# A retention layer feeding a gated two-layer block on one core: early loads of q, k, v put on another queue, and the first pairs' work reordered

## The chip, the cores and the metric

The kernel runs on one core of a Trainium2 chip. The core has five engines, each with its own queue that it works off in order: TensorE (PE, matrix products; its weight loads are shown apart as PEld), VectorE (DVE), ScalarE (ACT), GpSimd (POOL) and SyncE (SP, which only issues transfers here). Engines wait for each other through semaphores. Sixteen DMA engines carry the transfers of all queues. [...] The metric is the device time of one execution in microseconds, lower is better.

## What is computed

The inputs are q, k, v of shape (4, 8, 768, 64) and two weight matrices, all in float32. For each batch and head, a state is decayed and updated over 768 steps, and read with q. The result, 3072 tokens of 512 values, goes through two matrix products with an activation between them.

```python
gamma = 1.0 - 2.0 ** (-5.0 - np.arange(H))
for t in range(S):
    state = gamma * state + outer(k[:, :, t], v[:, :, t])
    y[:, :, t] = scale * (q[:, :, t] @ state)
x = y.transpose(0, 2, 1, 3).reshape(3072, 512)
h = x @ w_in            # 512 x 2048
g = h * np.cos(h)
out = g @ w_out         # 2048 x 512
```

## The kernel before, in words

The recurrence is done in chunks of 128 steps: six chunks for each batch entry. Two batch entries are worked side by side, which makes 12 **pairs** p = 0 to 11: pair p is chunk p mod 6 of batch entries b = 0 and 1 (p below 6) or 2 and 3. Two successive pairs give the 512 tokens of one **group** g of the block behind (six groups). "The second to fourth pairs" are p = 1, 2, 3.

A pair takes six loads of 256 KB: q0, q1, k0, k1, v0, v1 (the digit is b). `load` (L105) issues them on the queue that it is given, into five buffers for each (p mod 5). Then:

- `conv_q` (L150) and `conv_v` (L155) scale q and v with per-step factors and turn them to bfloat16, on the engine that they are given, two products a pair; `conv_k` (L160) copies k to bfloat16 on ACT, two copies a pair. There are three sets of buffers for these (p mod 3).
- `stage_t` (L167): PE transposes q and k (L176) into a PSUM bank for each b, and DVE or ACT copies the bank to `qkt` (L178, L180). From p = 5 on, transfers on SP do this instead (L186).
- `stage_a` (L196): PE makes the scores inside a chunk (L205). `stage_m` (L211, called by `masks`): DVE masks them into `am` (L214), four operations a pair.
- `stage_y` (L219): PE adds what the state gives (L228) and what the scores give (L233); ACT copies the result to `xt` (L237). Then PE updates the state (L245), and ACT or DVE copies it to `stb` (L250).

The block behind has `pair_f(p, r, parts)` (L272): for the 256 tokens of pair p and slice r of four, PE makes the first product in two halves of eight matmuls (L279); for each half, ACT takes the cosine into one of three buffers `cosb` (L258), and DVE multiplies into `gt` (L262). `parts` picks one half. Slice r needs slice r of w_in. From the third group on `unit_f` (L264) does the same for 512 tokens. `unit_o` (L288) is the second product, from `gt` and `w_out_sb`.

`load_w_in` (L114) and `load_w_out` (L119) load slices of the weights on POOL's queue, cast to bfloat16 on the way. Slice 0 of w_in is loaded in two parts of 256 columns, slices 1 to 3 as 512 columns each; w_out has four slices, which are all needed when `unit_o` begins.

Seven PSUM banks are taken and given back in rotation, one more is kept as `spare` for `warm(n)` (L313), which issues n matmuls that nobody reads, until `spare` is given to the rotation as well.

The schedule is manual: each engine works off its instructions in the order in which the program names them. Names follow the order of the code: L125 to L143 (first loads and constants), then L322 to L389 (the pairs 0 to 3 with all `pair_f`, written out by hand), then the loop at L393, in which `unit_f`, `unit_o` and the stages of pairs 4 to 11 alternate. A transfer reuses a semaphore that an earlier transfer of its queue had, and waits until that one has landed; there are eight for POOL's queue and eight for SP's.

Of the kernel before, what the change touches and what calls it, by code (L numbers as in the profile page):

```python
# [30 lines left out]
def kernel(  # L31
# [9 lines left out]
    nc = tc.nc  # L41
# [63 lines left out]
    def load(eng, p, names):  # L105
        bp, c = divmod(p, NC)
        for n in names:
            t, src = SRC[n[0]]
            b = int(n[1])
            eng.dma_start(  # L110
                out=t[p % PRE][b],
                in_=src[2 * bp + b, :, ds(c * C, C)].rearrange("h t d -> t h d"))

    def load_w_in(r, n=512):  # L114
        nc.gpsimd.dma_start(
            out=w_in_sb[:, :, ts(r, n)],
            in_=moe_w_in[:, ts(r, n)].rearrange("(i p) f -> p i f", p=128))

    def load_w_out(r):  # L119
        nc.gpsimd.dma_start(  # L120
            out=w_out_sb[:, ts(r, 4), :],
            in_=moe_w_out[ts(r, 512), :].rearrange("(f p) m -> p f m", p=128))
# [2 lines left out]
    nc.gpsimd.iota(pos, pattern=[[C, NC]], base=1, channel_multiplier=1,  # L125
                   allow_small_or_imprecise_dtypes=True)
    load(nc.sync, 0, ("q0", "k0", "q1"))
    load(nc.sync, 1, ("q0", "q1"))
    load(nc.gpsimd, 0, ("k1", "v0", "v1"))
    make_identity(nc, ident)  # L130
    nc.vector.memset(zero, 0.0)
# [15 lines left out]
    def bc(g, c):  # L147
        return g[:, c, :].unsqueeze(2).to_broadcast([128, H, D])

    def conv_q(p, eng):  # L150
        for b in range(2):
            eng.tensor_tensor(out=qs[p % NB][:, b], in0=qf[p % PRE][b],  # L152
                              in1=bc(gq, p % NC), op=ALU.mult)

    def conv_v(p, eng):  # L155
        for b in range(2):
            eng.tensor_tensor(out=vs[p % NB][:, b], in0=vf[p % PRE][b],  # L157
                              in1=bc(gk, p % NC), op=ALU.mult)

    def conv_k(p, on_act):  # L160
        for b in range(2):
            if on_act:
                nc.scalar.copy(out=ks[p % NB][:, b], in_=kf[p % PRE][b])  # L163
            else:
                nc.vector.tensor_copy(out=ks[p % NB][:, b], in_=kf[p % PRE][b])

    def stage_t(p, split, fill=0):  # L167
        n = p % NB
        for b in range(2):
            if fill:  # L170
                warm(fill * b)
            bank = banks.take()
            tr = bank.bitcast(BF16).rearrange("p (w a t) -> p w a t", w=2, a=HP)
            for w, src in enumerate((qs[n], ks[n])):
                for a in range(HP):
                    nc.tensor.transpose(tr[:, w, a, :], src[:, b, 2 * a : 2 * a + 2, :], ident)  # L176
            if split is None or split and b == 1:
                nc.vector.tensor_copy(out=qkt[n][:, :, b], in_=tr)  # L178
            else:
                nc.scalar.copy(out=qkt[n][:, :, b], in_=tr)  # L180
            banks.give(bank)
# [8 lines left out]
    def qt(n, b, a):  # L190
        return qkt[n][:, 0, b, a, :]

    def kt(n, b, a):
        return qkt[n][:, 1, b, a, :]

    def stage_a(p):  # L196
        n = p % NB
        todo = []
        for b in range(2):
            bk = [banks.take(), banks.take()]  # L200
            ap = [t.rearrange("p (a t) -> p a t", a=HP) for t in bk]
            for a in range(HP):
                for j in range(2):
                    po = 64 * j
                    nc.tensor.matmul(ap[j][:, a, :], lhsT=kt(n, b, a)[po : po + 64, :],  # L205
                                     rhs=qt(n, b, a)[po : po + 64, :],
                                     tile_position=(po, 0))
            todo.append((b, bk, ap))
        return todo

    def stage_m(p, item):  # L211
        b, bk, ap = item
        for j in range(2):
            nc.vector.tensor_tensor(  # L214
                out=am[p % 2][b][j], in0=ap[j],
                in1=mask.unsqueeze(1).to_broadcast([128, HP, 128]), op=ALU.mult)
            banks.give(bk[j])

    def stage_y(p, copy_st=nc.vector.tensor_copy):  # L219
        c = p % NC  # L220
        n = p % NB
        for b in range(2):
            bank = banks.take()
            yp = bank.rearrange("p (a t) -> p a t", a=HP)
            for a in range(HP):
                if c > 0:
                    for j in range(2):
                        nc.tensor.matmul(  # L228
                            yp[ts(j, 64), a, :], lhsT=stb[p % 2][:, b, a, ts(j, 64)],
                            rhs=qt(n, b, a), start=True, stop=False,  # L230
                            skip_group_check=True)
                for j in range(2):
                    nc.tensor.matmul(  # L233
                        yp[ts(j, 64), a, :], lhsT=vs[n][:, b, 2 * a + j, :],
                        rhs=am[p % 2][b][j][:, a, :], start=(c == 0), stop=True,
                        skip_group_check=True)
            nc.scalar.copy(out=xt[(p // 2) % 2][:, :, ts(2 * (p % 2) + b, C)], in_=yp)  # L237
            banks.give(bank)
        if c == NC - 1:
            return  # L240
        for b in range(2):
            for a in range(HP):
                for j in range(2):
                    h = 2 * a + j
                    nc.tensor.matmul(  # L245
                        st_ps[ts(j, 64), b, a, :], lhsT=ks[n][:, b, h, :],
                        rhs=vs[n][:, b, h, :], start=(c == 0 and b == 0 and a == 0),
                        stop=True, skip_group_check=True)
        for j in range(2):
            copy_st(out=stb[(p + 1) % 2][ts(j, 64), :, :, ts(j, 64)], in_=st_ps[ts(j, 64)])  # L250
# [4 lines left out]
    def act(bank, out):  # L255
        cb = cosb[f_no[0] % 3]
        f_no[0] += 1
        nc.scalar.activation(out=cb, in_=bank, func=AF.Sin, bias=halfpi)  # L258
        if len(out.shape) == 3:
            cb = cb.rearrange("p (f t) -> p f t", f=2)  # L260
            bank = bank.rearrange("p (f t) -> p f t", f=2)
        nc.vector.tensor_tensor(out=out, in0=bank, in1=cb, op=ALU.mult)  # L262
# [9 lines left out]
    def pair_f(p, r, parts=(0, 1)):  # L272

        g, hf = divmod(p, 2)
        for f in [4 * r + 2 * i for i in parts]:
            bank = banks.take()
            for e in range(2):
                for i in range(KIN):
                    nc.tensor.matmul(bank[:, ts(e, 256)], lhsT=w_in_sb[:, i, ts(f + e, 128)],  # L279
                                     rhs=xt[g % 2][:, i, ts(hf, 256)],  # L280
                                     start=(i == 0 and e == 0), stop=(i == KIN - 1),
                                     skip_group_check=True)
            act(bank, gt[g % 2][:, f : f + 2, ts(hf, 256)])
            banks.give(bank)
# [28 lines left out]
    def warm(n):  # L313
        for _ in range(n):
            nc.tensor.matmul(spare, lhsT=zero[:, :128], rhs=zero, start=True, stop=True,
                             skip_group_check=True)

    def masks(p, items):
        for it in items:
            stage_m(p, it)  # L320

    load(nc.gpsimd, 1, ("k0", "k1", "v0", "v1"))  # L322
    load_w_in(0, 256)
    load_w_in(1, 256)
    for r in (1, 2, 3):
        load_w_in(r)
    for p in (2, 3, 4):
        load(nc.sync, p, ("q0", "q1", "v0"))
    conv_v(1, nc.gpsimd)
    load(nc.gpsimd, 2, ("k0", "k1", "v1"))  # L330
    load(nc.gpsimd, 3, ("k0", "k1"))
    conv_q(2, nc.gpsimd)
    load(nc.gpsimd, 3, ("v1",))
    load_w_out(0)
    conv_v(2, nc.gpsimd)
    load_w_out(1)

    warm(10)
    conv_q(0, nc.vector)
# [7 lines left out]
    conv_q(1, nc.vector)  # L347
    warm(6)
    stage_y(0, nc.scalar.copy)
    conv_q(3, nc.gpsimd)  # L350
    load_w_out(2)
    load_w_out(3)
    conv_v(3, nc.gpsimd)
    load(nc.gpsimd, 4, ("k0", "k1", "v1"))
    stage_t(1, None)
    m1 = stage_a(1)
    masks(1, m1)
# [1 line left out]
    banks.give(spare)  # L359
    stage_y(1, nc.scalar.copy)  # L360
    pair_f(1, 0)
    for r in (1, 2, 3):
        pair_f(0, r)
        pair_f(1, r)
    conv_k(2, True)
    stage_t(2, None)
    m2 = stage_a(2)
    masks(2, m2)
    stage_y(2, nc.scalar.copy)
    load(nc.sync, 5, ("q0", "q1", "v0"))  # L370
    conv_q(4, nc.gpsimd)
    load(nc.gpsimd, 5, ("k0", "k1", "v1"))
    pair_f(2, 0)
    conv_k(3, True)
    pair_f(2, 1)
    stage_t(3, None)
    pair_f(2, 2, (0,))
# [15 lines left out]
    for g in range(1, NG + 1):  # L393
        for s in range(16):
            hf, r = divmod(s, 8)
            p = 2 * (g + 1) + hf
# [52 lines left out]
```

## Time and profile before

| what | value |
|---|---|
| runs | 219.2 to 222.09 us, median 219.92 (6 runs) |
| profiled execution | 220.12 us, its span 218.4 us |
| PE busy | 203.6 us (93%), 1699 matmuls |
| DVE / ACT / POOL busy | 113.4 / 116.2 / 83.8 us |
| DMA, hardware queue of SP and ACT | 54640 packets, 19.01 MB |
| DMA, software queue of POOL | 7712 packets, 13.90 MB |
| HBM read / written | 27.26 / 6.29 MB |
| PE busy in 34 to 41 us | 4.26 of 7.00 us |
| PE busy in 41 to 53 us | 10.47 of 12.00 us |
| PE busy in 65 to 218 us | 149.43 of 153.00 us |

The span runs from the first to the last instruction; times inside it are counted from its start. The landing of a transfer is the time at which its semaphore tells that all of it has arrived. Where each early transfer landed, in us (p and name; the queue is SP's where marked, else POOL's):

| transfer | landed |
|---|---|
| p=1: q0 (SP), q1 (SP), k0, k1, v0, v1 | 8.7, 10.9, 10.1, 11.7, 13.0, 13.9 |
| w_in, 256 columns, twice; slices 1, 2, 3 | 15.9, 18.1; 21.7, 25.1, 28.4 |
| p=2: q0, q1, v0 (all SP); k0, k1, v1 | 16.4, 22.4, 29.9; 30.1, 30.9, 31.7 |
| p=3: q0, q1, v0 (all SP); k0, k1, v1 | 37.5, 41.6, 42.3; 32.6, 33.4, 34.2 |
| w_out, slices 0 to 3 | 37.7, 41.3, 51.3, 54.7 |
| p=4: q0, q1, v0 (all SP); k0, k1, v1 | 43.2, 44.1, 45.4; 55.5, 56.3, 57.1 |

PE's own milestones: `pair_f(0, 0)` starts at 17.95, `pair_f(1, 0)` at 21.61, `pair_f(2, 0)` at 40.67, `pair_f(3, 0)` at 52.41 and the first `unit_o` at 59.39.

### The profile page before, as it was taken

What the parts mean: (1) busy time and instruction counts of PE and PEld (TensorE: products, weight loads), DVE (VectorE), ACT (ScalarE), POOL (GpSimd) and SP (SyncE); (2) the same over time, 40 slices, a digit from 0 to 9 for tenths busy, and PEclk for the clock granted to TensorE, in tenths of its full rate; (3) what the DMA queues carried; (4) which work ended last, traced back from release to release, by engine and by line L of the source; (5) the groups of instructions that cost most, each with busy time, mean ns of one, the idle gap of its engine ahead of it and who ended that gap; (6) DMA issues with size and microseconds to landing.
All of it is one profiled execution on the core that took longest, in us unless ns stands there. A gap on an engine that the chain in (4) does not pass through costs nothing.

```text
span 218.4 us, 4269 instructions
## 1 busy us (share of the span) xinstructions
PE 203.6 (93%) x1699; PEld 112.6 (52%) x1699; DVE 113.4 (52%) x183; ACT 116.2 (53%) x185; POOL 83.8 (38%) x96
## 2 busy tenths in 40 slices
PE   7578996889999999999999999999999999999992
PEld 2246884768855454544544544544544544444440
DVE  4398588386663417557448547647546244333000
ACT  5654874748874274564474564564534644454120
POOL 7988432499599953958070600000000000000000
PEclk9799999999999999999999999999999999999999
DMA  6999999899999999997972651051011001110221
GB/s 155 332 245 195 204 321 212 178 177 239 300 269 236 269 188 283 283 299 125 271 194 59 140 144 48 3 144 50 3 48 48 22 29 48 48 50 3 96 84 60
DMA packets 62516, 33.31 MB, mean 153 GB/s; under 512 B 52320, under 2 KB 57184, under 8 KB 62496
## 3 DMA queue, kind: packets, MB, share of 16 engines
q1 hardware_dynamic: 54640, 19.01, 37.8%
q0 software_dynamic: 7712, 13.90, 26.3%
q8 instruction: 13, 0.21, 0.4%
q10 hardware_dynamic: 144, 0.13, 0.2%
q14 instruction: 7, 0.06, 0.1%
HBM read 27.26 MB, written 6.29 MB: 154 GB/s over the span
## 4 chain that ended last, share of the span: by engine, by line
PE 83%; DVE 6%; ACT 5%; DMA 3%; issue 1%; SPq 0%; DVEq 0%; ACTq 0%
PE bank L293 37%; PE bank L267 26%; PE bank L279 11%; DMA qf<-in_q_dram 3%; PE bank L205 3%; DVE am L214 2%; PE bank L228 2%; PE bank L233 2%; ACT cosb L258 1%; ACT ks L163 1%; DVE qkt L178 1%; DVE qs L152 1%; ACT xt L237 1%; PE bank L176 1%; DVE gt L262 1%
## 5 line engine op out<-in xcount | busy, mean ns | idle before, releaser
L262 DVE TENSOR_TENSOR gt<-bank,cosb 128x512 bf16<-128x512 f32 x96 | 65.9, 690 | 70.0 <-ACT cosb L258 69.9
L258 ACT ACTIVATE cosb<-bank,halfpi 128x512 bf16<-128x512 f32 x96 | 65.8, 687 | 60.0 <-PE bank L267 49.9
L293 PE MATMUL bank<-w_out_sb,gt 128*128 128x512 bf16 x384 | 94.3, 379 | 0.0
L267 PE MATMUL bank<-xt,w_in_sb 128*128 128x512 bf16 x256 | 65.8, 379 | 0.0
L293 PEld LDWEIGHTS <-gt 128*128 128x128 bf16 x384 | 37.2, 98 | 44.3
L267 PEld LDWEIGHTS <-w_in_sb 128*128 128x128 bf16 x256 | 24.1, 98 | 28.3
L214 DVE TENSOR_TENSOR am<-bank,mask 128x512 bf16<-128x512 f32 x48 | 30.2, 682 | 5.9 <-PE bank L205 3.4
L152 POOL TENSOR_TENSOR qs<-qf,gq 128x512 bf16<-128x512 f32 x20 | 20.6, 1047 | 27.5 <-DMA qf<-in_q_dram 20.3
L279 PE MATMUL bank<-xt,w_in_sb 128*128 128x256 bf16 x256 | 28.9, 273 | 1.4 <-ACT xt L237 1.4
L157 POOL TENSOR_TENSOR vs<-vf,gk 128x512 bf16<-128x512 f32 x22 | 23.0, 1064 | 12.3 <-DMA vf<-in_v_dram 10.0
L279 PEld LDWEIGHTS <-w_in_sb 128*128 128x128 bf16 x256 | 24.8, 98 | 4.4 <-issue 1.3
L305 ACT COPY ob<-bank 128x512 f32<-128x512 f32 x23 | 13.5, 586 | 16.3 <-PE bank L293 16.1
L110 POOL DMA_DIRECT2D kf<-in_k_dram x23 | 20.9, 911 | 0.4 <-issue 0.4
L237 ACT CAST xt<-bank 128x512 bf16<-128x512 f32 x24 | 13.1, 588 | 14.7 <-PE bank L233 14.7
L163 ACT CAST ks<-kf 128x512 bf16<-128x512 f32 x24 | 13.7, 616 | 2.5 <-DMA kf<-in_k_dram 2.5
L233 PE MATMUL bank<-am,vs 128*64 128x128 bf16 x192 | 12.2, 219 | 1.2 <-DVE am L214 1.1
L110 POOL DMA_DIRECT2D vf<-in_v_dram x14 | 12.4, 888 | 0.0
L250 DVE CAST stb<-st_ps 64x512 bf16<-64x512 f32 x12 | 8.3, 689 | 6.5 <-PE st_ps L245 6.3
L233 PEld LDWEIGHTS <-vs 128*64 128x64 bf16 x192 | 10.3, 110 | 1.7 <-issue 0.9
L228 PEld LDWEIGHTS <-stb 128*64 128x64 bf16 x160 | 8.7, 109 | 4.5 <-issue 4.2
L228 PE MATMUL bank<-qkt,stb 128*64 128x128 bf16 x160 | 10.6, 222 | 0.0
L205 PE MATMUL bank<-qkt 64*128 64x128 bf16 x192 | 8.4, 223 | 2.3 <-DVE qkt L178 1.9
(37 smaller groups left out, 68.5 us busy)
## 6 DMA issues: line engine op xcount, KB each, us to landing
qf<-in_q_dram SPq DMA_DIRECT2D x24, 256.0 KB, 6.7
kf<-in_k_dram POOLq DMA_DIRECT2D x23, 256.0 KB, 5.7
out_dram<-ob SPq DMA_DIRECT2D x23, 256.0 KB, 2.2
vf<-in_v_dram POOLq DMA_DIRECT2D x14, 256.0 KB, 6.4
vf<-in_v_dram SPq DMA_DIRECT2D x10, 256.0 KB, 7.2
w_out_sb<-in_moe_w_out_dram POOLq DMA_DIRECT2D x4, 512.0 KB, 9.9
w_in_sb<-in_moe_w_in_dram POOLq DMA_DIRECT2D x3, 512.0 KB, 14.3
w_in_sb<-in_moe_w_in_dram POOLq DMA_DIRECT2D x2, 256.0 KB, 8.0
```

What stands on the lines that cost most here:

```text
L110: eng.dma_start(out=t[p % PRE][b], in_=src[2 * bp + b, :, ds(c * C, C)].rearrange("h t d -> t h d"))
L152: eng.tensor_tensor(out=qs[p % NB][:, b], in0=qf[p % PRE][b], in1=bc(gq, p % NC), op=ALU.mult)
L157: eng.tensor_tensor(out=vs[p % NB][:, b], in0=vf[p % PRE][b], in1=bc(gk, p % NC), op=ALU.mult)
L163: nc.scalar.copy(out=ks[p % NB][:, b], in_=kf[p % PRE][b])
L214: nc.vector.tensor_tensor(out=am[p % 2][b][j], in0=ap[j], in1=mask.unsqueeze(1).to_broadcast([128, HP, 128]), op=ALU.mult)
L228: nc.tensor.matmul(yp[ts(j, 64), a, :], lhsT=stb[p % 2][:, b, a, ts(j, 64)], rhs=qt(n, b, a), start=True, stop=False, skip_group_check=True)
L233: nc.tensor.matmul(yp[ts(j, 64), a, :], lhsT=vs[n][:, b, 2 * a + j, :], rhs=am[p % 2][b][j][:, a, :], start=(c == 0), stop=True, skip_grou ...
L258: nc.scalar.activation(out=cb, in_=bank, func=AF.Sin, bias=halfpi)
L262: nc.vector.tensor_tensor(out=out, in0=bank, in1=cb, op=ALU.mult)
L267: nc.tensor.matmul(bank, lhsT=w_in_sb[:, i, ts(f, 128)], rhs=xt[g % 2][:, i, :], start=(i == 0), stop=(i == KIN - 1))
L279: nc.tensor.matmul(bank[:, ts(e, 256)], lhsT=w_in_sb[:, i, ts(f + e, 128)], rhs=xt[g % 2][:, i, ts(hf, 256)], start=(i == 0 and e == 0), s ...
L293: nc.tensor.matmul(bank, lhsT=gt[g % 2][:, f, ts(j, 128)], rhs=w_out_sb[:, f, :], start=(f == 0), stop=(f == KOUT - 1))
```

## The change

```diff
     load(nc.sync, 0, ("q0", "k0", "q1"))
-    load(nc.sync, 1, ("q0", "q1"))
+    load(nc.sync, 1, ("q0", "v0"))
     load(nc.gpsimd, 0, ("k1", "v0", "v1"))
...
-    load(nc.gpsimd, 1, ("k0", "k1", "v0", "v1"))
+    load(nc.gpsimd, 1, ("k0", "q1", "k1", "v1"))
     load_w_in(0, 256)
     load_w_in(1, 256)
-    for r in (1, 2, 3):
-        load_w_in(r)
-    for p in (2, 3, 4):
-        load(nc.sync, p, ("q0", "q1", "v0"))
+    load_w_in(1)
+    load(nc.sync, 2, ("q0", "q1"))
+    load(nc.sync, 4, ("q0", "q1", "v0"))
     conv_v(1, nc.gpsimd)
-    load(nc.gpsimd, 2, ("k0", "k1", "v1"))
-    load(nc.gpsimd, 3, ("k0", "k1"))
+    load_w_in(2)
+    load(nc.gpsimd, 2, ("k0", "k1"))
+    load_w_in(3)
+    load(nc.gpsimd, 2, ("v0", "v1"))
+    load(nc.gpsimd, 3, ("k0", "q0", "k1", "q1"))
     conv_q(2, nc.gpsimd)
-    load(nc.gpsimd, 3, ("v1",))
-    load_w_out(0)
     conv_v(2, nc.gpsimd)
-    load_w_out(1)
+    load(nc.gpsimd, 3, ("v0", "v1"))
+    for r in range(4):
+        load_w_out(r)
...
     stage_y(0, nc.scalar.copy)
-    conv_q(3, nc.gpsimd)
-    load_w_out(2)
-    load_w_out(3)
     conv_v(3, nc.gpsimd)
     load(nc.gpsimd, 4, ("k0", "k1", "v1"))
+    warm(2)
     stage_t(1, None)
...
     pair_f(1, 0)
-    for r in (1, 2, 3):
+    for r in (1, 2):
         pair_f(0, r)
         pair_f(1, r)
     conv_k(2, True)
+    pair_f(0, 3)
     stage_t(2, None)
+    pair_f(1, 3, (0,))
     m2 = stage_a(2)
     masks(2, m2)
+    pair_f(1, 3, (1,))
     stage_y(2, nc.scalar.copy)
...
     pair_f(2, 0)
     conv_k(3, True)
+    conv_q(3, nc.vector)
     pair_f(2, 1)
     stage_t(3, None)
```

On SP's queue, v0 of p = 1 takes the place of q1, and behind q0, q1 of p = 2 stand those of p = 4 at once; v0 of p = 2 and q0, q1, v0 of p = 3 have left it. On POOL's queue, q1 of p = 1 and six loads of p = 2 and 3 are new or moved: k of p = 2 stands between slices 2 and 3 of w_in, `conv_v(1)` before slice 2, and the four slices of w_out stand behind all loads of p = 3. `conv_q(3)` goes from POOL to DVE, behind the products of `pair_f(2, 0)`. On PE, the last slice of `pair_f` for p = 0 and 1 is spread over the stages of p = 2: `pair_f(0, 3)` before the transposes, one half of `pair_f(1, 3)` before the scores and one before `stage_y(2)`. ACT's `conv_k(2)` and DVE's `gt` products move with them. Two `warm` matmuls are added ahead of the transposes of p = 1. What is computed is the same.

## The prediction

> **What bounds the kernel now.** I read the page's busy shares first: PE is busy for 203.6 of the 218.4 us span. So I asked for PE's waits by stage, then the chain of waits through the stage where they lie, then the timelines of DVE and POOL for prices. The profiled execution took 220.12 us, 1.72 around its span, and 0.20 above the median of 219.92. The waits of PE between 21.7 and 53 us (total, times, longest):
>
> ```profile
> PE bank L205 <- DVE qkt L178: 1.5, 4, 0.9
> PE bank L279 <- ACT xt L237: 1.4, 3, 0.5
> PE bank L176 <- ACT ks L163: 1.1, 1, 1.1
> PE bank L233 <- DVE am L214: 0.8, 2, 0.4
> ```
>
> And from 53 us to the end:
>
> ```profile
> PE bank L205 <- ACT qkt L180: 0.4, 1, 0.4
> ```
>
> No row names a DMA. After 21.7 us PE never waits for a transfer directly, and after 53 us it hardly waits at all, so whatever shift of PE the change makes by 53 us reaches the end whole. What can be won there is 4.8 us. The chain of waits (start, length, what) for pair p=2 shows where most of it sits:
>
> ```profile
> 34.03 0.69 ACT cosb L258
> 34.72 0.51 ACT ks L163
> ...
> 35.28 0.41 PE bank L176 x4
> ...
> 35.72 0.55 DVE qkt L178
> ...
> 36.32 0.61 DVE qkt L178
> ...
> 37.53 1.88 DVE am L214 x3
> ...
> 40.04 0.59 ACT xt L237
> ...
> 40.67 2.79 PE bank L279 x24
> ```
>
> PE has finished every pair_f of p=0 and 1 at 33.83, and then ACT, PE and DVE hand the work of p=2 to each other until pair_f(2, 0) starts at 40.67. Prices come from these rows of the timelines (start, length):
>
> ```profile
> 13.86 2.29 DVE L152 TENSOR_TENSOR qs<-qf,gq 128x512 bf16<-128x512 f32 x2
> ...
> 45.00 1.29 DVE L262 TENSOR_TENSOR gt<-bank,cosb 128x512 bf16<-128x512 f32 x2 [0.92 <-ACT cosb L258]
> 46.21 1.28 DVE L178 COPY qkt<-bank 128x1024 bf16<-128x1024 bf16 x2
> ```
>
> ```profile
> 13.12 2.49 POOL L157 TENSOR_TENSOR vs<-vf,gk 128x512 bf16<-128x512 f32 x2 [0.82 <-DMA vf<-in_v_dram]
> ```
>
> A pair of DVE operations takes 1.29, but conv_q(1) took 2.29 while POOL ran conv_v(1), which itself took 2.49 where two lone ones take 2.05.
>
> **The loads that move.** On the software queue a load lands every 0.8 us when queued (p=2 and 3, from 30.1 to 34.2 us). On SP the loads issued at 12.1 and 16.4 us needed 25.4 and 25.1, those issued by POOL in the same stretch 14.3 to 14.6: between 20 and 28 us the two queues moved nearly equal packet counts (1222 and 1218), but 1.41 MB against 0.31. So q of p=3, at 37.5 and 41.6 before, lands by about 35. [...] What must hold is that no load becomes late.
>
> q, v of p=1 swap queues: v0 takes q1's SP place (landed 10.9, on POOL before 13.0), q1 lands in k1's POOL place (11.7; needed by DVE at 13.9), k1 in v0's (13.0, before 11.7; conv_k(1) then ends at 13.6, its transposes are at 16.2). conv_v(1) starts 2 us earlier for b=0, but b=1 still waits for v1 at 13.9 and then meets conv_q(1) on DVE as before. I take 0, with −0.9 (no meeting) to +0.2 as ends. warm(2) adds two matmuls (six took 1.47 with their latency, so some 0.5) where PE now waits 0.83 for conv_q(1): free, or +0.2 if conv_q(1) gets quicker; inside the same ends.
>
> w_in(2) is issued after conv_v(1), at about 15 to 16 instead of 10.8 us; the queue is occupied until w_in(1) lands at 21.7, so it still lands at 25.1 (needed 26.9). w_in(3) now stands behind two loads of k. Rows: 3.3 to 3.6 per w_in slice, 0.8 per queued load, but 1.7 for the first load after a slice. So 25.1 + 1.6 + 3.3 = 30.0 at best, and 25.1 + 1.7 + 0.8 + 4.2 = 31.8 if the slice pays that 0.9 too. pair_f(0, 3) needs it at 30.34. The cover is conv_k(2), which now holds ACT just then: up to 30.8 nothing is lost, beyond it each us is one. So 0 to +1.0; I take 0, nearer to the other row of this kind (behind the last slice of w_out, landed at 54.66, the next k landed 0.86 later).
>
> POOL holds at most eight transfers in flight: w_out(0) waited 1.4 until w_in(2), issued eight places earlier, had landed (25.09), and went at 25.75. By that rule q1 of p=3 leaves after k0 of p=2 lands (about 26), so conv_q(2) runs at 27.5 to 29.6, needed at 32.1; conv_v(2) waits for v (31 to 33.6) and ends by 34.7, needed at 36.5; v of p=3 and the four w_out follow (4.9 us of issue), w_out lands by about 54 (needed 59.4); conv_v(3) ends between 39.6 and 41.4, needed at 49; loads of p=4 take 2.7 more, so conv_q(4) starts between 42.3 and 44.1.
>
> **Pair 2 on PE.** conv_k(2) moves ahead of the last four half-units' cosines. Half-units follow each other every 0.87 on PE; the cosine of the tenth after 21.6 us ends at 31.23, where in the old order the fourteenth's ended at 34.72: 3.49 earlier. conv_k(2) ends at 32.25 instead of 35.74. PE runs pair_f(0, 3) to 32.1 and the transposes to 33.0, without waiting. The cosines of pair_f(0, 3) follow conv_k on ACT at 32.15, so its first gt starts at 32.87. From there DVE has gt, gt, qkt, qkt, gt, am: exactly the series of p=3 before, where am began 3.00 after the first gt (45.00 to 48.00). So am starts at 35.87, and pair_f(2, 0) follows am by 3.75 as before (36.92 to 40.67): 39.62, that is **−1.05**. The two halves of pair_f(1, 3) lie in waits that stay.
>
> **Pair 3 on DVE.** conv_q(3) leaves POOL for DVE, between the gts of pair_f(2, 0) and of pair_f(2, 1). Counted from pair_f(2, 0): before, the second gt ended at 3.41 and the next began at 4.33, after conv_k(3) and a cosine. Alone, the two products take 1.29 and end at 4.62; with spacing 0.6 the next gt begins at 4.53, and qkt, A, am follow **+0.2** later. But they start at 39.62 + 3.33 = 42.95, and POOL's conv_q(4) lies between 42.3 and 46.2. If they meet as conv_q(1) and conv_v(1) did, DVE needs 2.29: **+1.0** more (0 if POOL starts after 44; 1.4 if it starts just before DVE, 0.65 of waiting and then another 1.04 between the two products, less what was idle). I take the meeting, since most of POOL's interval gives it. [...] Behind conv_q(3) on DVE wait gt of pair_f(2, 1), qkt and am of p=3, and PE waits at L205 for them; pair_f(2, 2) and (2, 3) keep their length. The old conv_q(3) on POOL (37.70 and 41.71) ended before PE needed it, so its removal gives PE nothing.
>
> Sum: 0 − 1.05 + 0 + 0.2 + 1.0 = +0.15, on the span 218.55, on the median 220.1.
>
> **Rivals.**
> No meeting: POOL's conv_q(4) is over or begins late; −0.85 gives 219.1, with pair 1's −0.9 also 218.2. For it: POOL's interval is guessed within 2 us. Against: DVE's 1.3 us lie well inside it.
> w_in(3) late, the slower side: it decides from 30.8 us on. At 31.8 it costs 1.0: 221.1; with the meeting's upper end 221.5; over 222.1 it needs a landing at 32.8. For it: the 1.7 row. Against: the 0.86 row.
> The clock: PE was busy for 1.26 us in the stretch 4.57 to 7.99, and the granted clock was 0.50 in the next 3.41. If p=3's longer wait does that, half of 3.41 is lost: 221.8. Against: 34.0 to 37.4 had 1.87 busy and kept 1.00.
> Pair 2's waits vanish: all 2.7 us of waits between 34 and 40.7 go and only the 0.2 remains: 217.4. Against: gt and qkt still queue on DVE behind conv_k.
> The loads do nothing for PE: contained in all of these, at 0.
>
> **How the numbers follow.** Within 1% (217.7 to 222.1) is about what counts as no change here. Chances: forecast 0.38 (own range 219.5 to 220.7), no meeting 0.25, w_in late 0.18 (0.07 of it beyond 222.1), clock 0.09 (0.05 beyond), waits vanish 0.10 (0.07 below 217.7). Faster 0.07, same 0.81, slower 0.12. The range 218.3 to 221.9 leaves out the vanishing waits (0.10) and the upper parts of w_in and clock (0.10).
>
> **What would show it.** pair_f(2, 0) at about 39.6 us; DVE's two L152 products at about 43 with 2.2 to 2.7 us for both, beside POOL's L152; no PE wait at pair_f(0, 3) for w_in; the interval from pair_f(2, 0) to pair_f(3, 0), 11.74 before, at 12.9. I am wrong if PE waits for a DMA after 21.7 us, if the clock drops again, or if PE's waits after 53 us grow.

## The result, and the profile after

The changed kernel takes 220.0 us (median of 35 runs, 219.18 to 225.56), the kernel before 220.11 in the runs taken beside it (72 runs). The ratio is 0.9995, with a 95% interval from 0.9978 to 1.0013: no change that can be measured, at 220.0 where 220.1 was forecast. The profiled execution has a span of 218.6 us. The ratios leave out executions more than 1.5% above the fastest of their kernel (4 of 12 of e4, 7 of 12 of e5), and since the profiled execution of e5 and of e6 is such a one, only its rows ahead of 53 us are read.

PE's waits between 21.7 and 53 us in the changed kernel (total, times, longest):

```profile
PE bank L176 <- DVE qs L152: 1.2, 2, 0.8
PE bank L205 <- DVE qkt L178: 1.0, 4, 0.3
PE bank L279 <- ACT xt L237: 0.9, 2, 0.5
PE bank L279 <- DMA w_in_sb<-in_moe_w_in_dram: 0.7, 1, 0.7
PE bank L233 <- DVE am L214: 0.6, 2, 0.4
```

And from 53 us on:

```profile
PE bank L205 <- DMA qkt<-ks: 0.7, 1, 0.7
PE bank L205 <- ACT qkt L180: 0.4, 1, 0.4
```

Before, the four rows of the first stretch came to 4.8 us. They count a wait of 0.5 for xt that ends at 21.61, just ahead of `pair_f(1, 0)`; the changed kernel's rows leave the same wait out, since it ends at 20.84 there. So 4.3 us stand against the 4.4 of the five rows now. The wait for ks of p=2 (1.1) and a third of those for qkt (1.5, now 1.0) are gone; a wait for DVE's products qs (1.2) and one for w_in (0.7) stand in their place. In the second stretch a wait for a transposing transfer has come that was not there.

The chain of waits (start, length, what) shows both sides of the trade, p=2 first and p=3 below it:

```profile
30.43 1.94 PE bank L279 x16
...
32.38 0.70 ACT cosb L258
...
33.10 0.69 DVE gt L262
33.80 1.11 DVE qkt L178 x2
...
35.51 2.48 DVE am L214 x4
...
39.26 1.92 PE bank L279 x16
...
42.66 2.04 DVE qs L152 x2
44.70 1.20 DVE gt L262 x2
45.90 1.21 DVE qkt L178 x2
...
52.02 1.03 PE bank L279 x8
```

`pair_f(2, 0)` starts at 39.26 where it started at 40.67, and the two products qs stand in the chain of p=3 with 2.04 us. The same in intervals, read from the starts of the L279 matmuls:

| stretch | before | after | difference |
|---|---|---|---|
| start of `pair_f(1, 0)` | 21.61 | 20.84 | −0.77 |
| to `pair_f(2, 0)` | 19.06 | 18.42 | −0.64 |
| to `pair_f(3, 0)` | 11.74 | 12.76 | +1.02 |
| to the first `unit_o` | 6.98 | 6.98 | 0 |
| to the end of the span | 159.02 | 159.57 | +0.55 |

The last row holds the wait of 0.72 at 84.14 us. The first row turns out below not to come from the change.

### The profile page after: what moved, and what is told of

It reads as the page before. It is cut to its first block, busy times and chain, and to the rows that moved or that the text cites. A ratio compares the mean times of both kernels' runs of the same rounds, so it can differ in the third digit from the quotient of the medians.

```text
span 218.6 us, 4276 instructions
## 1 busy us (share of the span) xinstructions
PE 204.8 (94%) x1701; PEld 112.2 (51%) x1701; DVE 115.0 (53%) x185; ACT 116.2 (53%) x185; POOL 86.4 (40%) x98
## 4 chain that ended last, share of the span: by engine, by line
PE 70%; DMA 15%; DVE 5%; ACT 4%; POOL 3%; SPq 1%; issue 1%; DVEq 0%; ACTq 0%; POOLq 0%
PE bank L293 34%; PE bank L267 25%; DMA w_in_sb<-in_moe_w_in_dram 5%; DMA qkt<-ks 5%; PE bank L279 5%; DMA vf<-in_v_dram 4%; PE bank L205 2%; PE bank L233 2%; PE bank L228 2%; DVE gt L262 2%; ACT cosb L258 2%; POOL vs L157 1%; SPq L110 1%; DVE am L214 1%; DVE qkt L178 1%
## 5 line engine op out<-in xcount | busy, mean ns | idle before, releaser
L279 PE MATMUL bank<-xt,w_in_sb 128*128 128x256 bf16 x256 | 29.5, 273 | 2.1 <-ACT xt L237 1.4
L152 POOL TENSOR_TENSOR qs<-qf,gq 128x512 bf16<-128x512 f32 x18 | 19.1, 1079 | 23.8 <-DMA qf<-in_q_dram 18.4
L279 PEld LDWEIGHTS <-w_in_sb 128*128 128x128 bf16 x256 | 24.6, 98 | 5.4 <-issue 1.3
L237 ACT CAST xt<-bank 128x512 bf16<-128x512 f32 x24 | 13.0, 588 | 10.9 <-PE bank L233 10.9
L110 POOL DMA_DIRECT2D vf<-in_v_dram x15 | 13.4, 893 | 0.0
```

The lines of the kernel that those rows point to most:

```text
L110: eng.dma_start(out=t[p % PRE][b], in_=src[2 * bp + b, :, ds(c * C, C)].rearrange("h t d -> t h d"))
```

## The experiments

All ratios are to the kernel before, in runs on the same chip. "Interval 2" is from `pair_f(1, 0)` to `pair_f(2, 0)`, "interval 3" from there to `pair_f(3, 0)`.

**e1: conv_q(3) back on POOL.**

```diff
     stage_y(0, nc.scalar.copy)
+    conv_q(3, nc.gpsimd)
     conv_v(3, nc.gpsimd)
...
     conv_k(3, True)
-    conv_q(3, nc.vector)
     pair_f(2, 1)
```

> The changed kernel with conv_q(3) put back on POOL, ahead of conv_v(3). Theory (the two products on DVE meet POOL's conv_q(4) and cost about 1.0, the longer series on DVE 0.2): the interval from pair_f(2, 0) to pair_f(3, 0) falls from 12.76 to about 11.74, and the time by about 1.0 us (ratio to before about 0.995). Rival A (POOL is the scarce engine, DVE has room): the interval stays at 12.5 or more, because transposes of p=3 now wait for POOL. Rival B (what costs is the wait of 0.72 us for a transposing transfer at 84 us, made by the new order of the queues): that wait is here too and the total does not fall.

The starts of `pair_f(2, 0)` and `pair_f(3, 0)` in its PE timeline (start, length, what):

```profile
39.37 3.65 PE L279 MATMUL bank<-xt,w_in_sb 128*128 128x256 bf16 x32 [0.42 <-ACT xt L237]
...
51.10 3.11 PE L279 MATMUL bank<-xt,w_in_sb 128*128 128x256 bf16 x27 [0.47 <-ACT xt L237]
```

Measured: interval 3 is 11.73, interval 2 is 18.02, ratio 0.9937 (0.9906 to 0.9967). The time falls as the theory said. Rival A falls with interval 3. The wait for qkt<-ks is in this profile too, with 2.5 us, and yet the runs are faster: Rival B falls as the explanation of what conv_q(3) costs.

**e2: conv_q(4) on POOL later, conv_q(3) stays on DVE.**

```diff
-    conv_q(4, nc.gpsimd)
     load(nc.gpsimd, 5, ("k0", "k1", "v1"))
+    conv_q(4, nc.gpsimd)
```

> The changed kernel with conv_q(4) on POOL issued after the three loads of p=5 instead of ahead of them; conv_q(3) stays on DVE. Theory (the meeting, not DVE's place in the series): DVE's two products take about 1.3 instead of 2.1, the interval from pair_f(2, 0) to pair_f(3, 0) falls from 12.76 to about 11.9, the time by 0.8 us. Rival (the two products cost their own 1.3 us on DVE whoever runs beside them): their rows stay at about 2.1 or the interval stays at 12.7.

DVE's timeline in the changed kernel (start, length, what):

```profile
42.58 2.13 DVE L152 TENSOR_TENSOR qs<-qf,gq 128x512 bf16<-128x512 f32 x2
44.63 1.28 DVE L262 TENSOR_TENSOR gt<-bank,cosb 128x512 bf16<-128x512 f32 x2
```

POOL's timeline there:

```profile
42.95 2.65 POOL L152 TENSOR_TENSOR qs<-qf,gq 128x512 bf16<-128x512 f32 x2
```

And DVE's in e2, where POOL's products begin at 48.51:

```profile
42.94 1.29 DVE L152 TENSOR_TENSOR qs<-qf,gq 128x512 bf16<-128x512 f32 x2
44.14 1.28 DVE L262 TENSOR_TENSOR gt<-bank,cosb 128x512 bf16<-128x512 f32 x2
```

The same two products on the same engine take 2.13 beside POOL's and 1.29 alone, so the meeting costs 0.84. Interval 3 is 11.92 in e2, 0.84 below the changed kernel and 0.19 above e1: the 0.19 is what the place on DVE costs. Ratio 0.9966 (0.9927 to 1.0006), not clear of 1 by itself; interval 2 is 18.78 here, since the last slice of w_in landed later (30.74) and PE waited 1.05 for it.

**e3: the order of the loads alone.** The diff of the loads as in the change; PE, DVE and ACT as before, conv_q(3) on POOL ahead of conv_v(3), no added `warm`.

> The kernel before with the changed order of the loads alone (PE, DVE and ACT in the old order, no added warm, conv_q(3) on POOL). Theory (no wait of PE names a transfer, so loads alone give nothing): pair_f(1, 0) to pair_f(2, 0) takes about 19.1 as before, plus 0 to 0.7 if PE waits for the last slice of w_in at 30 us, which has no cover here; time between 0 and +0.7 us against before. Rival (the loads carry the gain): interval below 18.7 and time below before by 0.5 us or more.

Its waits of PE from 20.7 to 53 us hold, among others:

```profile
PE bank L176 <- ACT ks L163: 1.1, 1, 1.1
PE bank L279 <- DMA w_in_sb<-in_moe_w_in_dram: 1.0, 1, 1.0
```

Interval 2 is 20.61: 1.55 more than before, of which 1.0 is the wait for the last slice of w_in, all of it lost, and the rest comes with a stretch of half clock from 37.5 to 40.9 us (granted clock 0.58 from 37 to 40, 0.85 from 40 to 43). That is more than I allowed for. Interval 3 is 11.73. Ratio 1.0025 (0.9989 to 1.0061). The loads alone bring nothing.

**e4: the order of p=2 alone.** Loads and queues as before.

```diff
-    for r in (1, 2, 3):
+    for r in (1, 2):
         pair_f(0, r)
         pair_f(1, r)
     conv_k(2, True)
+    pair_f(0, 3)
     stage_t(2, None)
+    pair_f(1, 3, (0,))
     m2 = stage_a(2)
     masks(2, m2)
+    pair_f(1, 3, (1,))
```

> The kernel before with the spread of pair_f(0, 3) and pair_f(1, 3) over the stages of p=2 alone (loads, queues and conv_q(3) as before). Theory: pair_f(1, 0) to pair_f(2, 0) takes 1.05 less than before, about 18.0, with no wait for w_in; pair_f(2, 0) to pair_f(3, 0) stays at 11.7; time about 1.0 us below before. Rival (the new order needs the earlier loads): PE or ACT waits for k or v of p=2 (landed 30.9 and 31.7 before), the interval stays at 18.6 or more and the time within 0.4 of before.

Interval 2 is 18.02, 1.04 below before; PE's table names neither ks nor w_in:

```profile
PE bank L205 <- DVE qkt L178: 2.1, 4, 0.9
PE bank L279 <- ACT xt L237: 0.9, 2, 0.5
PE bank L233 <- DVE am L214: 0.6, 2, 0.4
```

Interval 3 is 11.73. Ratio 0.9927 (0.9889 to 0.9965): these few lines are better than the whole change, and the late loads of k and v of p=2 in the old order do not hold them up.

**A second profile of the kernel before.**

> The kernel before, profiled a second time. Theory (pair_f(1, 0) started 0.77 earlier in the changed kernel's profile because the stretch of half clock fell elsewhere, not because of the change): here too pair_f(1, 0) starts anywhere between 20.7 and 21.7 us, by where the stretch at clock 0.50 begins; the two intervals behind it stay at 19.06 and 11.7. Rival (the swap of q1 and v0 of p=1 gave it): pair_f(1, 0) at 21.6 again, whatever the clock does.

`pair_f(1, 0)` starts at 20.86, where it had started at 21.61 in the first profile and starts at 20.84 in the changed kernel. The stretch at clock 0.50 began at 9.6 here, at 8.0 in the first profile, at 10.1 in the changed kernel. So the 0.77 of the table is not the change's, and the rival (the swap of q1 and v0) falls. But the intervals did not stay: 19.41 and 13.39. The windows of this profile (stretch, length, PE busy, instructions, granted clock, share of the DMA engines, GB/s) say why:

```profile
34.00:37.00 3.00, 1.98 (x31) 0.98 1.23 233
37.00:40.00 3.00, 2.54 (x46) 0.50 1.25 218
40.00:43.00 3.00, 2.76 (x14) 0.50 0.87 168
```

From 36.9 to 43.7 us the clock was at half, in the lull of p=2, and both intervals together are 2.0 us longer than in the first profile.

**Two more profiles of the changed kernel.**

> The changed kernel, profiled a second time. Theory (the wait for qkt<-ks at 84 us comes from a gap in the transfers that some executions have): no such wait, or of another length; intervals 18.4 (18.0 to 18.8, by how late w_in lands) and 12.7. Rival (the new order of the queues makes it): 0.7 us or more again at 84 us.

> The changed kernel, profiled a third time, beside the others on this chip. Theory: a wait for qkt<-ks at 84 us of 0.5 us or more, as in the two looks before (0.72, 2.59). Rival (chance): no wait.

Interval 2 is 18.39 and 18.60, with waits for w_in of 0.67 and 0.87; interval 3 is 12.76 and 12.89. The wait for qkt<-ks came again, with these rows in the two profiles:

```profile
PE bank L205 <- DMA qkt<-ks: 2.6, 1, 2.6
```

```profile
PE bank L205 <- DMA qkt<-ks: 0.5, 1, 0.5
```

So that wait is in all three profiles of the changed kernel, with 0.5 to 2.6 us. It is in that of e1 too (2.5), and not in those of e2, e3, e4 or in either of the kernel before. e3 has the changed order of the loads, so that order alone does not make it.

**e5: e4 with conv_v(1) behind the loads of p=2.**

```diff
-    conv_v(1, nc.gpsimd)
     load(nc.gpsimd, 2, ("k0", "k1", "v1"))
+    conv_v(1, nc.gpsimd)
```

> The kernel of e4 (the order of p=2 alone) with conv_v(1) on POOL put behind the three loads of p=2 instead of ahead of them. Theory (conv_q(1) on DVE meets conv_v(1) on POOL as conv_q(3) met conv_q(4)): DVE's two L152 products at 13 us take about 1.3 instead of 2.1, and pair_f(0, 0) could start up to 0.8 earlier; its second half needs the second slice of w_in, landed at 17.9, so a gain remains only where pair_f(0, 0) would start after 17.0. Interval from pair_f(1, 0) to pair_f(2, 0) 18.0 as in e4; time 0 to 0.8 below e4's ratio of 0.993. Rival (vs of p=1 comes too late for stage_y(1)): PE waits for POOL's L157 before pair_f(1, 0).

In its profile the meeting was not avoided. DVE:

```profile
13.48 4.11 DVE L152 TENSOR_TENSOR qs<-qf,gq 128x512 bf16<-128x512 f32 x2
```

and POOL:

```profile
13.99 0.96 POOL L110 DMA_DIRECT2D vf<-in_v_dram  x1
14.89 2.13 POOL L157 TENSOR_TENSOR vs<-vf,gk 128x512 bf16<-128x512 f32 x2
```

DVE's second product began at 14.08 and ended at 17.58, after POOL's last. Interval 2 is 18.01. The ratio of 0.9901 (0.9864 to 0.9937) overlaps that of e4: whether the later place gains anything stays open.

**e6: the last slice of w_in ahead of k of p=2.**

```diff
-    load(nc.gpsimd, 2, ("k0", "k1"))
     load_w_in(3)
+    load(nc.gpsimd, 2, ("k0", "k1"))
```

> The changed kernel with the last slice of w_in issued ahead of k of p=2 instead of behind it. Theory (conv_k(2) on ACT covers some 0.3 us of a late slice, the rest is lost, and k of p=2 would now be late): no PE wait for w_in at 30 us, but k lands at 29.7 to 31.3 and ACT waits for it, so the interval from pair_f(1, 0) to pair_f(2, 0) is 18.0 to 18.6 against 18.4. Rival (the late slice costs its whole 0.7 and k has room): interval below 17.9.

Interval 2 is 18.04, 0.38 below the changed kernel, without a wait for w_in; PE waited 0.3 for POOL's qs of p=2, which had moved back, and not for k. The theory's size holds at its lower end, its reason (k late) does not. DVE's two products took 3.22 us here, against 2.13 in the changed kernel, and interval 3 was 13.85. Ratio 0.9988 (0.9953 to 1.0024).

**e7 and e8: loads of p=7 ahead.** On the changed kernel (e7) and on e4 (e8):

```diff
     load(nc.gpsimd, 6, ("k0", "k1", "v1"))
+    load(nc.gpsimd, 7, ("k0", "k1", "v1"))
...
-                        load(nc.gpsimd, p + 3, ("k0", "k1", "v1"))
+                        if p > 4:
+                            load(nc.gpsimd, p + 3, ("k0", "k1", "v1"))
```

> The changed kernel with POOL's three loads of p=7 issued directly behind those of p=6, so that they no longer run beside the transposing transfers of p=6 (issued at 71 to 75 us). Theory (the transposes land late because software-queue loads run beside them): the transposes of p=6 land within 7 us of their issue instead of 11, PE does not wait for qkt<-ks at 84 us, and the time falls by the mean of that wait, 0.5 to 1.5 us below the changed kernel (ratio 0.993 to 0.997). Rival (the gap comes by chance in either order of queues): the wait may be there or not, and the ratio stays at 0.998 to 1.001.

> The same kernel as e7_k7_early, profiled again: theory, no wait for qkt<-ks at 84 us again; rival, a wait of 0.5 us or more in one of the two.

> The kernel of e4 (the order of p=2 alone on the kernel before) with the same move of the loads of p=7. Theory: nothing is lost at p=2 and 3 (intervals 18.0 and 11.7), no wait at 84 us, and the best time of all: ratio 0.990 to 0.993. Rival (e4 had no such wait to lose): ratio 0.993 as for e4, or worse if POOL's products of p=5 come late behind the added loads.

Neither profile of e7 has the wait, but the transposes of p=6 still took 6.7 to 9.6 us to land, and the ratio is 1.0 (0.9965 to 1.0036): taking the wait away gained nothing that the runs show. The expectation also had the wrong loads beside these transposes. In the changed kernel's profile the loads of p=7 were issued from 63.9 us on and had all landed by 71.4, when the first of the transposes was issued; beside them run the loads of p=8 (from 70.6) and p=9 (from 77.3), and e7 leaves both there (from 71.9 and 78.6). So e7 does not test whether such loads delay the transposes. e8 has 0.9925 (0.9899 to 0.9951), intervals 18.01 and 11.73, and no wait, like e4. So e1, e4 and e8 are about 0.7% below the kernel before, with intervals that overlap each other, and e4 is there without the early loads of p=7.

## Why the prediction was right

| term | predicted | measured |
|---|---|---|
| loads by themselves | 0 | no gain (e3) |
| p=1, swap and `warm` | 0 | about 0 (20.84 against 20.86 in the second profile before) |
| p=2, order | −1.05 | −1.04 (e4) |
| last slice of w_in | 0, up to +1.0 | +0.4 (18.42 against 18.02) |
| p=3, place on DVE | +0.2 | +0.19 (e2 against e1) |
| p=3, the meeting | +1.0 | +0.84 (changed against e2) |
| behind 53 us | 0 | a wait of 0.5 to 2.6 in the three profiles |
| sum up to `pair_f(3, 0)` | +0.15 | +0.38 (−0.64 + 1.02) |

The mechanism held: a gain on PE at p=2 that a loss on DVE at p=3 gives back. The two were shown apart, by e4 and by e1 and e2. Of the signs that the prediction named, `pair_f(2, 0)` (39.6 forecast) came at 39.26, and interval 3 (12.9) was 12.76; the two products on DVE, at 2.13 beside POOL's 2.65, were just short of the 2.2 to 2.7. But PE did wait for w_in, and its waits after 53 us grew: two of the three things by which the prediction would have called itself wrong.

Two sizes were off. The slice of w_in landed at 30.38, within the 30.0 to 31.8 that the rows gave, and the extra 0.9 of a changeover was not paid (25.49, then 26.28 and 27.10 for k, then 30.38). But PE wanted it at 29.7, not 30.3, since `pair_f(1, 0)` came 0.77 earlier, in an execution with its early half clock from 10.1 us instead of 8.0; and the cover behind conv_k(2) is 0.3, not 0.45: waits of 0.20, 0.69, 0.87 and 1.05 (e1, the changed kernel, its third profile, e2) gave intervals of 18.02, 18.42, 18.60 and 18.78. The meeting was 0.84, since I took it from 2.29 in the old p=1, where POOL's products and DVE's lay otherwise.

Three steps were wrong without moving the sum. The 4.8 us that "can be won" were 4.3, as said above. I had v0 of p=1 land at 10.9 in q1's place on SP, and conv_v(1) start 2 us earlier for it; it landed at 12.75, and POOL waited for it:

```profile
12.89 2.98 POOL L157 TENSOR_TENSOR vs<-vf,gk 128x512 bf16<-128x512 f32 x2 [2.09 <-DMA vf<-in_v_dram]
```

And I wrote that any shift of PE by 53 us reaches the end whole: in the changed kernel's profiles the wait for qkt<-ks takes part of it back. Its cause stays open. In that stretch, from 75 to 81 us, the DMA engines were nearly as busy as before (1.11 against 1.17) and moved less than half (length, granted clock, share of the DMA engines, GB/s), first the kernel before, then the changed one:

```profile
75.00:81.00 6.00, 1.00 1.17 206
```

```profile
75.00:81.00 6.00, 1.00 1.11 80
```

with transposes and software-queue loads in flight together in both. e7 does not settle it: it has no wait in two profiles, but kept loads beside the transposes, and its runs are not faster.

Of the rivals, "no meeting" and "waits vanish" fall by the 2.13 us and by the 4.4 us of waits that remained; the late slice came in part (+0.4). The clock fell on the other kernel: in the old order's lull, to 0.50 from 36.9 to 43.7 us in the second profile of the kernel before and from 37.5 to 40.9 in e3. With the new order of p=2 the granted clock was 1.00 from 34 to 43 us in the changed kernel, in its second profile and in e4, and its mean over the whole execution was 0.999 in the third profile and 1.0 in the first of e7.

The lists of the runs, which give each one's mean granted clock, tell more. One stretch of 3.41 us at half clock lowers the mean over 218 us by 0.008. Of the runs that the ratios count, 39 of the 78 listed for the kernel before are below 0.987, with a median of 221.2 us, and 4 of the 33 of the changed kernel. At 0.987 and above the medians are 219.85 (39 runs) and 219.95 (29). There e4 has 218.83 (8 runs) against 219.88 for the kernel before on the same chip (16): the order of p=2 is worth 1.05 us at like clock too. The 78 and the 33 were not run side by side, and the lists do not tell where in a run the clock fell.

So the number came out closer than its parts. Three things that the sum had at 0 moved: the slice (+0.4), the tail (0.4 to 2.4 us longer in the three profiles, 159.40 to 161.45 against 159.02), and, the other way, the clock, which the old order lost more often. That they nearly cancel in the medians is luck; how much each adds to an average run is not shown.

Of the meeting the rows show the sizes alone: DVE's two products took 1.29 with none of POOL's beside them (e2), and beside POOL's 2.13 in the changed kernel, 2.29 in the old p=1 and 4.11 in e5. What passes between the two engines meanwhile, no run here shows.

## What to carry to other kernels

Work that fills a wait pays only as far as the engine that ends the wait next has room: here ACT finished conv_k(2) 3.49 us earlier (10.64 instead of 14.13 us after the start of `pair_f(1, 0)`, in e4), DVE's queue let 1.04 of it reach PE, and that size could be read from a series of operations that the trace already had one stage later. Before moving an elementwise product to an idle-looking engine, look at what the engine beside it runs at that very moment; the price of the meeting stood in the old trace, at another stage (2.29 us beside POOL's products, where a pair of DVE operations takes 1.29). The loads that no wait of PE named brought nothing here by landing earlier (e3), and putting them ahead of a slice that PE did need cost it up to 1.05 us of waiting.

## What was not expected of the hardware

The clock fell in the middle of the kernel without an idle stretch. In the second profile of the kernel before, PE was busy for 1.89 of the 3.41 us ahead of the fall at 36.9, and the clock was 0.50 for 6.8 us; in e3 it was busy for 1.88 of the 3.41 us ahead of the fall at 37.5, with 1.06 for its longest wait, and the clock was 0.50 for 3.4 us. In the first profile of the kernel before it was busy for 1.87 from 34.0 to 37.4, and the clock stayed at 1.00 to 40.8. The same share came with both, so it does not decide by itself. The early falls do not come in every execution either: the first profile of the changed kernel was at 0.50 from 10.10 to 13.51, after 1.42 busy in the 3.41 us ahead, while its second profile and the first of e7 have a mean granted clock of 1.0. What makes the clock fall is not shown.

The transposing transfers issued at 62.0 and 63.4 us in the changed kernel took 3.0 and 2.8 us to land, and those issued at 71.4 and 72.8 took 11.1 and 11.3. Loads of the software queue were in flight beside both; no run here shows what made the difference.
